# One attention-and-FFN decode step: 64 rows of w_down in one load of eight partitions

## The chip, the cores and the metric

The kernel runs on one core of a Trainium2 chip. The metric is the device time of one execution in microseconds (us), as the median of several runs; lower is better. Times inside an execution come from one profiled run: they count from the start of its span, which is the time from the first to the last instruction.

A core has five engines that work side by side and wait for each other by semaphores: PE (matmul; its weight loads are listed as PEld), DVE (vector), ACT (scalar), POOL (GpSimd) and SP (Sync). All large loads of this kernel are issued by SP and carried by the core's 16 DMA engines, which take them in the order in which SP issued them.

## The reference

One token passes a grouped-query attention over a long cache and then a gated FFN, each with a layer norm in front and a residual behind.

```python
def _A_ref(x, k_cache, v_cache, wq, wo):       # 32 query heads, 4 KV heads, 65536 cached keys, head size 128
    q = (x @ wq) ...                           # D = 1024
    scores = jnp.einsum("bhqd,bhkd->bhqk", q, k) * (Dh ** -0.5)
    p = _softmax(scores, axis=-1)
    o = jnp.einsum("bhqk,bhkd->bhqd", p, v)
    return o... @ wo
def _B_ref(x, w_gate, w_up, w_down):           # F = 3584
    return (_gelu(x @ w_gate) * (x @ w_up)) @ w_down
h  = x + _A_ref(_layernorm(x), k_cache, v_cache, wq, wo)
h2 = h + _B_ref(_layernorm(h), w_gate, w_up, w_down)
```

All tensors are bf16. The caches are 64 MB each, and the five weight matrices 8, 8, 7, 7 and 7 MB.

## The kernel before

**The loads.** Everything that is streamed goes through one SBUF tile, `ring`, of three slots with 32768 bf16 elements on each partition. `load` (line 172) takes the next slot, or a place behind the last load in the same slot when it is given an offset, and issues one DMA on SP (line 179). In order there are `wq`, sixteen loads of the caches, `wo`, `w_gate`, `w_up`, and then `w_down` in five pieces that share one slot. By the count of slots, `wo` and `w_down` use the same slot, and `w_gate` the one after it. A load may not start before the matmuls that read the old contents of its place are done; so the pieces of `w_down` wait for the matmuls of `wo`.

**The layout of w_down.** `w_down` has 3584 rows of 1024 elements. The view `wd_v` puts 28 consecutive rows (FC = 28) on each of 128 partitions. A piece is a range of these 28 places: 16 of them, then 8, then 3; the last place is loaded as two halves of 512 columns, a DMA each, 128 KB over 128 partitions, so 1 KB on each.

**The FFN's activation.** `act_bf` (line 544) holds the 3584 hidden values, 28 on each partition. `padded` (line 235) copies them into `actz`, a tile of [128, 28, 32] that POOL has set to zero, at column 0 of each group of 32, so that a stationary operand is 128 rows by 32 columns with one column that is not zero.

**The first 16 places.** `row_mm` (line 468) multiplies one place with a row of 1024 columns of `w_down`: two matmuls of 512 columns, at one of four column groups of the array (place modulo 4). They add to `at_ps`, the two PSUM banks in which the attention's output and the residual are already summed. Matmuls on four column groups run side by side.

**The end.** `rows_out("sum_r")` copies the two banks to SBUF, DVE one and ACT the other. Eight matmuls with `ones_f` then add the four column groups and lay the result out as eight pieces of 128 columns, in `f_ps` and `fb_ps` (`half_mm`, line 566). The 8 places, the 3 places and the last place are multiplied by `down_rows` (line 570) and added in the same two tiles, in matmuls of 128 columns. After the first half of the last place DVE copies `f_ps` out, after the second ACT copies `fb_ps`, and SP writes the result.

**Fillers.** `keep_busy(n, src)` (line 557) issues n matmuls of 128x128 by 512 columns into `w_ps`, which nobody reads. There are 4 before the first piece of `w_down`, 3 after its 16 places, 4 after the eight matmuls with `ones_f`, and 3 after the 8 places.

**Order.** The framework orders each engine's instructions by a simulation when the kernel is built. `mm` (line 153) passes each matmul through `keep` (line 135), which ties it behind the last one, so PE runs its matmuls in written order. The DMAs of `load`, the POOL instructions and those DVE and ACT instructions that are not wrapped in `dv` or `ac` have no such tie. `seen_by_sync` makes SP wait for the listed loads before the output is written.

```python
for c in range(c0):                                               # c0 = 16
    row_mm(at_ps, actz[:, c, :], wv[:, c, :], c, False, c + 4 >= c0)
keep_busy(3, wv[:, 0, 0:512])
sum_r = rows_out("sum_r")
...
for sz, nb in ((8, 3), (3, 0)):
    wv = load(wd_v[:, c0:c0 + sz, :], c0 * D)
    down_rows(wv, c0, sz, [0, 1])
...
```

Of the kernel before, what the change touches and what calls it, by code (L numbers as in the profile page):

```python
# [9 lines left out]
ALU = mybir.AluOpType  # L10
AX = mybir.AxisListType
BF16 = mybir.dt.bfloat16
F32 = mybir.dt.float32
PSUM = bass.MemoryType.PSUM
# [3 lines left out]
def kernel(  # L18
# [13 lines left out]
    nc = tc.nc  # L32
    P = 128
    D = A_x.shape[-1]
# [4 lines left out]
    F = B_w_gate.shape[1]  # L39
    DC = D // P  # L40
    FC = F // P
# [5 lines left out]
    CW = 16384  # L47
    NSLOT = 3
# [25 lines left out]
    sel = lead.tile([P, 32], F32, name="sel")  # L74
# [12 lines left out]
    ring = chpool.tile([P, NSLOT * 2 * CW], BF16, name="ring")  # L87
    top = ctx.enter_context(tc.tile_pool(name="top", bufs=1))
# [3 lines left out]
    def pt_tile(i, shape, dtype, name):  # L92
        return (lead if i == 0 else top).tile(shape, dtype, name=name, tag=f"pT{i}")
# [50 lines left out]
    def pe(op):  # L144
        return keep(op, "pe")
# [7 lines left out]
    def mm(out, lhsT, rhs, start, stop, loaded=False, tile_position=None, skip_group_check=False):  # L153
        t = nc.tensor
        if not loaded:
            return pe(t.matmul(out, lhsT=lhsT, rhs=rhs, start=start, stop=stop, tile_position=tile_position,  # L156
                               skip_group_check=skip_group_check))
        op = t.add_instruction(mybir.InstMatmult(  # L158
            name=nc.get_next_instruction_name(), engine=t.engine, start_tensor_calc=start, stop_tensor_calc=stop,
            tile_size=(lhsT.shape[0], lhsT.shape[1]), tile_position=tile_position or (0, 0), ldweights=False,  # L160
            bass_skip_group_check=skip_group_check,
            ins=[t.lower_ap(rhs), t.lower_ap(lhsT, for_matmul_weights=True)], outs=[t.lower_ap(out, opt=True)]))
        reuses.add(op.ins.name)
        return pe(op)
# [4 lines left out]
    slot = [NSLOT - 1]  # L169
    loads, pools, last = [], [], {}  # L170

    def load(src, off=0):
        n, w = src.shape[1], src.shape[2]
        if off == 0:
            slot[0] = (slot[0] + 1) % NSLOT
        assert off + n * w <= 2 * CW
        o = slot[0] * 2 * CW + off
        tv = ring[:, o:o + n * w].rearrange("p (n w) -> p n w", w=w)
        loads.append(nc.sync.dma_start(out=tv, in_=src).ins)
        return tv  # L180
# [20 lines left out]
    for bp in range(4):  # L201
        s0 = 64 * (bp // 2) + bp % 2
        nc.vector.tensor_copy(out=esel[:, bp, :, :],
                              in_=ident_bf[:, s0:s0 + 63:2].unsqueeze(1).to_broadcast([P, 4, 32]))

    one = ctx.enter_context(tc.tile_pool(name="one", bufs=1))
# [28 lines left out]
    def padded(i, vec, ncols, name):  # L235
        t = pt_tile(i, [P, ncols, 32], BF16, name)
        pools.append(nc.gpsimd.memset(t[:], 0.0))
        nc.vector.tensor_copy(out=t[:, :, 0], in_=vec)
        return t
# [7 lines left out]
    def evac(dst, src, k):  # L247
        return nc.vector.tensor_copy(out=dst, in_=src) if k % 2 == 0 else nc.scalar.copy(out=dst, in_=src)
# [161 lines left out]
    for n, u in enumerate(units):  # L410
# [24 lines left out]
        if g == 0 and li == NL - 1:  # L435
            softmax_turn(0)
            softmax_bias(0)
            for i, m in zip((NL - 1, 0, 1, 2), (2, 3, 4, 4)):
# [11 lines left out]
                            pattern=[[-1, OQ], [1, P]], channel_multiplier=-OQ)  # L450
# [8 lines left out]
    actx.close()  # L459
    ps_a = ctx.enter_context(tc.tile_pool(name="ps_a", bufs=2, space=PSUM))  # L460
    ps_w = ctx.enter_context(tc.tile_pool(name="ps_w", bufs=2, space=PSUM))
    ps_f = ctx.enter_context(tc.tile_pool(name="ps_f", bufs=1, space=PSUM))
    DS = D // 512

    def row_bank(name):
        return ps_w.tile([P, 512], F32, name=name, tag="w")

    def row_mm(banks, stat, w2, c, first, last):
        g = c % 4
        for s in range(DS):  # L470
            mm(banks[s][32 * g:32 * g + 32, :], stat, w2[:, s * 512:(s + 1) * 512], first, last,
               loaded=(s > 0), tile_position=(0, 32 * g), skip_group_check=True)
# [4 lines left out]
    at_ps = [ps_a.tile([P, 512], F32, name="at_ps", tag="a") for _ in range(DS)]  # L477
    wv = load(wo_v[:])
# [7 lines left out]
    def rows_out(name):  # L486
        t = low.tile([P, DS, 512], F32, name=name, tag="sc0")
        for s in range(DS):
            last["act"] = evac(t[:, s, :], at_ps[s][:], s)
        return t  # L490
# [18 lines left out]
    def turned(banks, name, tag):  # L509
# [2 lines left out]
            nc.vector.transpose(out=t[:, k, :], in_=banks[k][:, 0:HF * 32])  # L512
        return t[:].rearrange("p k (j i) -> p (k j) i", i=32)[:, :, 0]

    g_banks = [row_bank("wg_ps") for _ in range(2)]
    gv = B_w_gate.rearrange("(p c) n -> p c n", c=DC)
    uv = B_w_up.rearrange("(p c) n -> p c n", c=DC)
# [25 lines left out]
    act_bf = top.tile([P, FC], BF16, name="act_bf")  # L543
    nc.vector.tensor_tensor(out=act_bf[:], in0=turned(u_banks, "wu_t", "sc2"), in1=gl[:], op=ALU.mult)

    wd_v = B_w_down.rearrange("(p c) n -> p c n", p=P)
    actz = padded(3, act_bf[:], FC, "actz")
    w_ps = row_bank("w_ps")

    def seen_by_sync(ins):  # L550
        seen = nc.sync.nop()
        for i in ins:
            tc.add_manual_dep(seen.ins, i.name,
                              mybir.DependencyInfo(mybir.DependencyClass.Sync, mybir.DependencyReason.DATA),
                              reason="seen")

    def keep_busy(n, src):
        for i in range(n):
            mm(w_ps[:], ident_bf[:], src, True, True, loaded=(i > 0))

    HW = D // 2
# [8 lines left out]
    def down_rows(wv, c0, n, bs):  # L570
        for cc in range(n):
            c = c0 + cc
            for g in range(4):
                for b in bs:
                    o = (b if len(bs) > 1 else 0) * HW + g * QW
                    half_mm(b, g, actz[:, c, :], wv[:, cc, o:o + QW], False, c + 1 == FC, loaded=(b > bs[0]))

    keep_busy(4, wu[:, 0, 0:512])
    c0 = 16
    wv = load(wd_v[:, 0:c0, :])  # L580
    for c in range(c0):
        row_mm(at_ps, actz[:, c, :], wv[:, c, :], c, False, c + 4 >= c0)
    keep_busy(3, wv[:, 0, 0:512])
    sum_r = rows_out("sum_r")
    for g in range(4):
        for b in range(2):
# [2 lines left out]
    for sz, nb in ((8, 3), (3, 0)):  # L589
        wv = load(wd_v[:, c0:c0 + sz, :], c0 * D)  # L590
# [3 lines left out]
    assert c0 == FC - 1  # L594
    o_b = o_fin[:].rearrange("p (b j) -> p b j", b=2)
    for b, put in ((0, nc.vector.tensor_copy), (1, nc.scalar.copy)):
        wv = load(wd_v[:, c0:FC, b * HW:(b + 1) * HW], c0 * D + b * HW)
        down_rows(wv, c0, 1, [b])
        if b == 1:
            seen_by_sync(loads[-8:] + [last["act"].ins] + [x.ins for x in pools])  # L600
        put(out=o_b[0:97, b, :], in_=halves[b][0:97, :])
    nc.sync.dma_start(out=out[0, 0].rearrange("(b g n) -> g b n", b=2, g=4),
                      in_=o_b[0:97:32, :, :])
# [30 lines left out]
```

## Time and profile before

| | |
|---|---|
| median of three runs | 407.71 us (407.51 to 408.35) |
| the profiled execution | 407.8 us, of which the span is 406.0 us |
| mean granted PE clock | 0.891 of full speed |
| busy: PE, DVE, ACT, POOL | 295.5, 203.8, 40.0, 7.5 us |
| read from HBM | 173.02 MB, 426 GB/s over the span |
| loads of `w_down`: issued | 355.95 us and the 3.6 us after it, five DMAs |
| issue to landing: 16, 8 and 3 places, each half | 39.6, 43.6, 45.0 and 44.8 us |

The time outside the span, 1.8 us, lies before the first and after the last instruction. A matmul's row gives its start and a modelled end; matmuls overlap, so the distance between starts says more than the duration. The granted clock tells how fast PE was allowed to run in a stretch: 1.00 is full speed and 0.50 half.

### The profile page before, as it was taken

How to read it: one execution, taken by the hardware profiler on the slowest of the kernel's cores; microseconds unless marked ns; L12 is line 12 of the kernel's file. 1: busy time of each engine (PE TensorE's matmuls, PEld its weight loads, DVE VectorE, ACT ScalarE, POOL GpSimd, SP SyncE). 2: the span in 40 equal slices, each digit the busy share in tenths (PEclk: the TensorE clock that was granted, in tenths of full speed). 3: DMA queues.
4: the chain of work that ended last, by engine and by line, in shares of the span. 5: the costliest groups of instructions: out<-in, count | busy, mean ns of one | idle time of the engine just before them, and what ended most of it. 6: DMA issues, size and time to landing. Idle time of an engine off the chain costs nothing.

```text
span 406.0 us, 2610 instructions
## 1 busy us (share of the span) xinstructions
PE 295.5 (73%) x1519; PEld 59.4 (15%) x681; DVE 203.8 (50%) x186; ACT 40.0 (10%) x62; POOL 7.5 (2%) x17
## 2 busy tenths in 40 slices
PE   0160777758899695979969957997696999646196
PEld 0110111111111110221111113111110211211012
DVE  0210989999839744971595387609943000220210
ACT  1000000023000031100000302000021100100000
POOL 2000000000000000000000000000010000000000
PEclk9995689987899999769999967899999699886689
DMA  9999999999999999999999999999999999999995
GB/s 413 413 413 471 458 413 415 413 466 452 413 421 420 471 439 413 428 420 471 433 420 428 420 465 433 420 435 420 458 433 420 441 420 458 399 442 447 400 423 225
DMA packets 3631, 173.18 MB, mean 427 GB/s; under 512 B 416, under 2 KB 676, under 8 KB 804
## 3 DMA queue, kind: packets, MB, share of 16 engines
q1 hardware_dynamic: 3612, 173.02, 98.7%
q8 instruction: 8, 0.13, 0.1%
q14 instruction: 3, 0.02, 0.0%
q10 hardware_dynamic: 8, 0.00, 0.0%
HBM read 173.02 MB, written 0.00 MB: 426 GB/s over the span
## 4 chain that ended last, share of the span: by engine, by line
DMA 41%; PE 35%; DVE 21%; ACT 2%; issue 1%; ACTq 0%; DVEq 0%
DMA ring<-in_A_k_cache_dram 30%; DVE ring L288 16%; PE acc_ps L158 16%; DMA ring<-in_B_w_down_dram 11%; PE qk_ps L156 6%; PE qk_ps L158 5%; PE acc_ps L156 5%; DVE mx L313 2%; ACT sc L309 2%; DVE pT L346 1%; PE o_ps L156 1%; PE at_ps L156 1%; DVE acc_sb L369 1%; PE at_ps L158 1%; PE nb_ps L156 0%
## 5 line engine op out<-in xcount | busy, mean ns | idle before, releaser
L288 DVE STREAM_TRANSPOSE ring<-ring 128x2048 uint32<-128x2048 uint32 x64 | 142.6, 2279 | 36.9 <-DMA ring<-in_A_k_cache_dram 36.9
L156 PE MATMUL qk_ps<-ring,wsel 128*128 128x512 bf16 x256 | 107.4, 420 | 50.2 <-DVE ring L288 31.2
L158 PE MATMUL qk_ps<-ring,wsel 128*128 128x512 bf16 x256 | 106.6, 416 | 0.0
L158 PE MATMUL acc_ps<-ring,pT 128*128 128x512 bf16 x384 | 105.1, 383 | 0.0
L156 PEld LDWEIGHTS <-wsel 128*128 128x128 bf16 x256 | 27.1, 106 | 157.3 <-issue 140.4
L156 PE MATMUL acc_ps<-ring,pT 128*128 128x512 bf16 x128 | 49.1, 384 | 0.0
L313 DVE TENSOR_REDUCE mx<-qk_ps 128x1 f32<-128x1024 f32 x16 | 19.5, 1220 | 24.7 <-ACT sc L309 18.7
L346 DVE STREAM_TRANSPOSE pT<-pT 128x1024 bf16<-128x1024 bf16 x16 | 19.3, 1228 | 23.8 <-ACT pT L340 23.8
L309 ACT COPY sc<-qk_ps 128x1024 f32<-128x1024 f32 x12 | 12.1, 1012 | 149.5 <-PE qk_ps L158 149.5
L156 PEld LDWEIGHTS <-pT 128*128 128x128 bf16 x128 | 12.8, 100 | 90.7 <-issue 90.6
L369 DVE COPY acc_sb<-acc_ps 32x512 f32<-32x512 f32 x8 | 5.3, 667 | 29.4 <-PE acc_ps L158 29.3
L340 ACT ACTIVATE pT<-sc,nbias 128x1024 bf16<-128x1024 f32 x12 | 13.7, 1141 | 44.9 <-DVE nbias L332 41.9
L156 PE MATMUL wu_ps<-ring,hnz 128*32 128x448 bf16 x32 | 5.9, 729 | 9.0 <-DMA ring<-in_B_w_up_dram 9.0
L156 PE MATMUL ln_tot<-ln_s,ones_f 128*128 128x1 f32 x8 | 1.9, 312 | 13.5 <-DVE ln_s L210 11.7
L156 PE MATMUL q_ps<-ring,xnz 128*32 128x512 bf16 x32 | 5.0, 598 | 8.9 <-DMA ring<-in_A_wq_dram 8.9
L156 PE MATMUL wg_ps<-ring,hnz 128*32 128x448 bf16 x32 | 5.9, 718 | 7.2 <-DMA ring<-in_B_w_gate_dram 7.2
L156 PE MATMUL o_ps<-sel,acc_sb 128*128 128x8 f32 x32 | 6.6, 335 | 5.8 <-DVE rl L383 5.4
L371 ACT COPY acc_sb<-acc_ps 32x512 f32<-32x512 f32 x8 | 4.6, 578 | 58.6 <-DVE acc_sb L369 58.5
L512 DVE STREAM_TRANSPOSE wu_t<-wu_ps 128x448 f32<-128x448 f32 x2 | 1.2, 630 | 14.2 <-PE wu_ps L156 14.2
L261 DVE STREAM_TRANSPOSE q_t<-q_ps 128x512 f32<-128x512 f32 x2 | 1.3, 694 | 13.8 <-PE q_ps L158 13.8
L512 DVE STREAM_TRANSPOSE wg_t<-wg_ps 128x448 f32<-128x448 f32 x2 | 1.2, 628 | 13.4 <-PE wg_ps L156 13.4
L340 ACT ACTIVATE pT<-qk_ps,nbias 128x1024 bf16<-128x1024 f32 x4 | 4.5, 1114 | 29.8 <-PE acc_ps L158 16.8
(108 smaller groups left out, 94.2 us busy)
## 6 DMA issues: line engine op xcount, KB each, us to landing
ring<-in_B_w_gate_dram SPq DMA_DIRECT2D x1, 7168.0 KB, 35.5
ring<-in_B_w_up_dram SPq DMA_DIRECT2D x1, 7168.0 KB, 38.6
ring<-in_B_w_down_dram SPq DMA_DIRECT2D x1, 4096.0 KB, 39.6
ring<-in_B_w_down_dram SPq DMA_DIRECT2D x1, 2048.0 KB, 43.6
ring<-in_B_w_down_dram SPq DMA_DIRECT2D x1, 768.0 KB, 45.0
ring<-in_B_w_down_dram SPq DMA_DIRECT2D x2, 128.0 KB, 44.8
ring<-in_A_k_cache_dram SPq DMA_DIRECT2D x8, 38.6
ring<-in_A_v_cache_dram SPq DMA_DIRECT2D x8, 34.4
```

The costliest lines, as they stand in the source:

```text
L156: return pe(t.matmul(out, lhsT=lhsT, rhs=rhs, start=start, stop=stop, tile_position=tile_position, skip_group_check=skip_group_check))
L158: op = t.add_instruction(mybir.InstMatmult(name=nc.get_next_instruction_name(), engine=t.engine, start_tensor_calc=start, stop_tensor_calc ...
L261: nc.vector.transpose(out=q_t[:, k, :], in_=q_banks[k])
L288: dv(nc.vector.transpose(out=kt[:, c * w:(c + 1) * w], in_=kt[:, c * w:(c + 1) * w]))
L309: ac(nc.scalar.copy(out=sc[:], in_=flat))
L313: dv(nc.vector.tensor_reduce(out=state[("mx", g)][:, li:li + 1], in_=flat, axis=AX.X, op=ALU.max))
L340: ac(nc.scalar.activation(out=flat, in_=state.pop(("sc", g, li)), func=ACT.Exp, bias=st["nbias"][:, 0:1], scale=scale, accum_out=st["lpart ...
L346: dv(nc.vector.transpose(out=flat, in_=flat))
L369: dv(nc.vector.tensor_copy(out=acc_sb[sl, :], in_=acc[sl, c, :]))
L371: ac(nc.scalar.copy(out=acc_sb[sl, :], in_=acc[sl, c, :]))
L512: nc.vector.transpose(out=t[:, k, :], in_=banks[k][:, 0:HF * 32])
```

## The change

The last place of each partition, 128 rows of `w_down`, is split. The rows of the 64 even partitions stay in the two half-row loads, which now write every second partition (`wv[0:P:2]`). The rows of the 64 odd partitions come in one new DMA: they go to eight partitions (0, 8, ... 56), eight rows of 2 KB on each, 128 KB in all, into the first 8192 elements of the slot after that of `w_down`, which is the slot of `w_gate`. In the program text this DMA stands after the 16 places and before the load of the 8.

The hidden values of the odd partitions must follow their rows. Two small masks are made of `sel`: `part` (which of eight rows a partition's value belongs to) and `even`. `spread`, a 128x128 matrix of ones and zeros, is made on POOL; a matmul of it with `act_q` (the mask times the last hidden value) puts the 64 values onto the eight partitions, in `act_ps`, in a new PSUM pool. `few` is the padded copy of it, and eight `row_mm` multiply it with the eight rows of `lv`, adding to `at_ps` before `sum_r`. In `actz`, the last place is multiplied with `even`.

```diff
+    ps_s = ctx.enter_context(tc.tile_pool(name="ps_s", bufs=1, space=PSUM))
...
+    low_rows = B_w_down.rearrange("(q r c) n -> q r c n", q=KQ, c=2 * FC)[:, :, 2 * FC - 1, :]
...
+    nc.vector.tensor_reduce(out=part[:], in_=sel[:].rearrange("p (x r t) -> p t r x", r=KR, t=2)[:, 1], axis=AX.X, op=ALU.add)
+    nc.vector.tensor_reduce(out=even[:], in_=sel[:, 0::2], axis=AX.X, op=ALU.add)
+    nc.gpsimd.memset(spread[:], 0.0)
+    ones_at = spread[:, 0:8 * KQ:8]
+    nc.gpsimd.memset(ones_at, 1.0)
+    nc.gpsimd.affine_select(out=ones_at, ...)
+    nc.gpsimd.affine_select(out=ones_at, ...)
...
-    actz = padded(3, act_bf[:], FC, "actz")
+    actz = pt_tile(3, [P, FC, 32], BF16, "actz")
+    pools.append(nc.gpsimd.memset(actz[:], 0.0))
+    nc.vector.tensor_copy(out=actz[:, 0:FL, 0], in_=act_bf[:, 0:FL])
+    act_q = one.tile([P, KR], BF16, name="act_q", tag="ln_xc")
+    nc.vector.tensor_tensor(out=act_q[:], in0=part[:], in1=act_bf[:, FL:FC].to_broadcast([P, KR]), op=ALU.mult)
+    nc.vector.tensor_tensor(out=actz[:, FL, 0:1], in0=even[:], in1=act_bf[:, FL:FC], op=ALU.mult)
...
     for c in range(c0):
-        row_mm(at_ps, actz[:, c, :], wv[:, c, :], c, False, c + 4 >= c0)
+        row_mm(at_ps, actz[:, c, :], wv[:, c, :], c, False, False)
+    act_ps = ps_s.tile([P, KR], F32, name="act_ps")
+    mm(act_ps[:], spread[:], act_q[:], True, True)
+    few = padded(1, act_ps[:], KR, "few")
+    at = (slot[0] + 1) % NSLOT * 2 * CW
+    lv = ring[:, at:at + KR * D].rearrange("p (r n) -> p r n", n=D)
+    loads.append(nc.sync.dma_start(out=lv[0:8 * KQ:8], in_=low_rows).ins)
     keep_busy(3, wv[:, 0, 0:512])
+    for r in range(KR):
+        row_mm(at_ps, few[:, r, :], lv[:, r, :], r, False, r + 4 >= KR)
     sum_r = rows_out("sum_r")
...
-        wv = load(wd_v[:, c0:FC, b * HW:(b + 1) * HW], c0 * D + b * HW)
+        o = slot[0] * 2 * CW + c0 * D + b * HW
+        wv = ring[:, o:o + HW].rearrange("p (c n) -> p c n", c=1)
+        loads.append(nc.sync.dma_start(out=wv[0:P:2], in_=wd_v[0:P:2, c0:FC, b * HW:(b + 1) * HW]).ins)
...
-            seen_by_sync(loads[-8:] + [last["act"].ins] + [x.ins for x in pools])
+            seen_by_sync(loads[-9:] + [last["act"].ins] + [x.ins for x in pools])
```

KQ and KR are 8, FL is 27. The bytes read from HBM are the same as before.

More of the change, by code (lines that the diff above doesn't have):

```diff
@@ L513, in turned @@
         return t[:].rearrange("p k (j i) -> p (k j) i", i=32)[:, :, 0]
+    KQ = 8
+    KR = P // 2 // KQ
+    KW = P // KQ
+    assert KQ * KR * 2 == P and 2 * KR == KW and KR * D <= DC * F
+    low_rows = B_w_down.rearrange("(q r c) n -> q r c n", q=KQ, c=2 * FC)[:, :, 2 * FC - 1, :]
+    part = one.tile([P, KR], F32, name="part", tag="gmb")
+    even = top.tile([P, 1], F32, name="even")
+    spread = top.tile([P, P], BF16, name="spread", tag="wo")
+    nc.vector.tensor_reduce(out=part[:], in_=sel[:].rearrange("p (x r t) -> p t r x", r=KR, t=2)[:, 1], axis=AX.X, op=ALU.add)
[3 more added lines that the diff above has]
+    nc.gpsimd.memset(ones_at, 1.0)
+    nc.gpsimd.affine_select(out=ones_at, in_=ones_at, compare_op=ALU.is_ge, fill=0.0, base=0,
+                            pattern=[[-KW, KQ]], channel_multiplier=1)
+    nc.gpsimd.affine_select(out=ones_at, in_=ones_at, compare_op=ALU.is_ge, fill=0.0, base=KW - 1,
+                            pattern=[[KW, KQ]], channel_multiplier=-1)
     g_banks = [row_bank("wg_ps") for _ in range(2)]
@@ L546 @@
     wd_v = B_w_down.rearrange("(p c) n -> p c n", p=P)
-    actz = padded(3, act_bf[:], FC, "actz")
+    FL = FC - 1
+    actz = pt_tile(3, [P, FC, 32], BF16, "actz")
[4 more added lines that the diff above has]
+    nc.vector.tensor_tensor(out=actz[:, FL, 0:1], in0=even[:], in1=act_bf[:, FL:FC], op=ALU.mult)
     w_ps = row_bank("w_ps")
```

## The prediction

> **What bounds the kernel now.** I read the page, then the chain of work that ended last, the timeline of the last 11 us, the waits, the timelines of POOL and SP, and the windows. The DMA engines are busy nearly all the span; the chain's last link is a load of w_down (start, duration):
>
> ```profile
> DMA  9999999999999999999999999999999999999995
> ...
> 358.13 44.71 DMA ring<-in_B_w_down_dram
> ```
>
> It landed at 402.84. The timeline of PE (start, us, operation) shows what was done meanwhile:
>
> ```profile
> 395.56 0.41 PE L156 MATMUL at_ps<-ring,actz 128*32 128x512 bf16 x4 [0.26 <-DMA ring<-in_B_w_down_dram]
> ...
> 397.07 0.41 PE L158 MATMUL at_ps<-ring,actz 128*32 128x512 bf16 x4
> 397.41 0.39 PE L156 MATMUL w_ps<-ring,ident_bf 128*128 128x512 bf16 x1
> ...
> 398.27 0.45 PE L156 MATMUL f_ps<-sum_r,ones_f 128*32 128x128 f32 x8
> ...
> 398.87 0.39 PE L156 MATMUL w_ps<-ring,ident_bf 128*128 128x512 bf16 x1
> ...
> 400.41 0.24 PE L156 MATMUL f_ps<-ring,actz 128*32 128x128 bf16 x4 [0.51 <-DMA ring<-in_B_w_down_dram]
> ...
> 401.43 0.39 PE L156 MATMUL w_ps<-ring,ident_bf 128*128 128x512 bf16 x1
> ...
> 402.23 0.24 PE L156 MATMUL f_ps<-ring,actz 128*32 128x128 bf16 x4
> ...
> 402.88 0.24 PE L156 MATMUL fb_ps<-ring,actz 128*32 128x128 bf16 x4
> ```
>
> PE begins each piece 0.04 us after it landed (395.52, 400.37, 402.19, 402.84 by the trace's semaphore records) and fills the time between with fillers. Its spare time is small: the fillers from 398.87 would let the 8 places start at about 399.89 instead of 400.41 (0.52 us spare), those from 401.43 end as the 3 places land (none), and before the last half some 0.25 us are spare. After 402.88 the copy, the output and the end of the span take 3.1 us, in any version.
>
> The second reading is how instruction streams are ordered. Two answers, POOL and SP:
>
> ```profile
> 340.39 0.31 POOL L237 MEMSET hnz<- 128x256 bf16 x1 [5.95 <-PE acc_ps L158]
> 347.30 0.84 POOL L237 MEMSET actz<- 128x896 bf16 x1 [6.59 <-PE acc_ps L158]
> 362.13 0.56 POOL L226 TENSOR_TENSOR ln_rstd<-ln_ve,neg_half 128x1 f32<-128x1 f32 x1 [13.98 <-DVE ln_ve L224]
> ...
> 355.95 3.58 SPq L179 DMA_DIRECT2D ring<-in_B_w_down_dram x5
> ```
>
> The second layer norm's power (called at line 503) is written before the memsets of `hnz` (504) and `actz` (547), yet both run earlier, at 340 and 347, each when its buffer came free. So an engine's stream is in order of readiness, not of the text, where nothing ties it. PE is tied; SP's DMAs are not. All five pieces left together, as the matmuls of wo (352.61 to 357.4) freed their places.
>
> **The change, part by part.** *Masks and `spread`*: two DVE reduces (0.16 to 0.23 us each, by lines 195 and 210), and on POOL two memsets (0.21 and 0.1), two selects (0.30 each, by the identity's) and the memset of `few` (0.31). POOL is idle for 14.0 us before 362.13 and DVE for 13.4 before 376.58. Nothing; without that cover they would delay the layer norm by 1.2 us, still inside PE's 7.2 us wait for w_gate. *Two multiplies on DVE* after `actz` (0.2 each): if the first 16 places waited for them too, PE would start at 395.75, +0.2 at most. One more semaphore in SP's last wait: nothing, its load is used 5 us earlier.
>
> *PE's new work*: after 397.07 come a 128x8 matmul, the old three fillers beside the copy to `few` (DVE, 0.25 by the copies at 351.63 and 352.26, from 0.26 after the matmul), and 16 matmuls of 512 columns, four groups of 0.215 us. `sum_r` waits for the last.
>
> *The two halves*: 64 packets of 1 KB each instead of 128. The old halves landed 0.34 us apart, so each takes 0.17 less; 0.34 in sum.
>
> *The new load* decides. Its place is the slot of w_gate: its first 8192 elements were read by w_gate's first three chunks, about 369.0 to 371.9. The 8 places, the 3 places and the halves, written after it, are ready at about 357, when the matmuls of wo are done. By the POOL rows, SP's stream gets them first: 16, 8, 3, half, half, and the new load last, issued after 371.9 but behind all of w_down in the DMA engines. PE, tied to the text, reaches the new rows at about 398.3 and stands there, with the 8, the 3 and the halves unread behind it.
>
> When does it land? A DMA engine carries 16 KB of it if eight engines share it: a 16 KB packet took 0.61 us in the trace's packet records, two old halves 0.68; I take 0.65. With the 0.34 saved that is 0.31 after the old last half on the same engine. That half's sixteen increments came in two groups, seven at 400.71 to 401.39 and nine at 402.30 to 402.84. So it lands at 401.7 if its engines are all early ones, 403.15 if the latest is among them; I take 403.0, since nine of sixteen are late. Before, the load of x_row into four partitions left eight packets (four of data, four increments), so I take it that eight partitions mean eight engines. A rule of the Trainium skill speaks against this load: "SBUF — State Buffer", Door 1, puts partitions 0 and 32, 8 and 40 and so on onto shared ports, so that eight partitions reach four. No row here shows that; by it the load would take twice as long and land at 403.7.
>
> From there PE is alone on the path. First new matmul 403.04; to the start of the last group 0.65; to the matmuls with ones 1.20 (397.07 to 398.27); those 0.60; four fillers 1.02 (398.87 to 399.89); the 8 places 1.02 (400.41 to 401.43); three fillers 0.80; the 3 places 0.34 and one half 0.06. Sum 5.69: the last half starts at 408.73 instead of 402.88, +5.85 us.
>
> *The clock*: PE then idles from 398.2 to 403.0. The windows (us; PE, PEld, DVE, ACT, POOL busy; granted clock; DMA share; GB/s):
>
> ```profile
> 375.90:379.31 3.41, 1.01 (x12) 0.00 (x0) 2.26 (x8) 0.23 (x1) 0.00 (x0) 1.00 1.09 471
> 386.14:389.55 3.41, 3.41 (x24) 0.51 (x12) 0.00 (x0) 0.00 (x0) 0.00 (x0) 0.50 1.00 432
> ```
>
> Clock steps lie on a grid of 3.41 us: after a window with 1.01 us of PE the clock halved at 379.31, and the full window to 389.55 brought it back. The window 399.8 to 403.2 would be almost empty, so the new matmuls run at half speed. If that lasts to 406.6, the rows, the copy's start and the ones cost about 1.3 us more; if to 410.0 (the window to 406.6 would hold some 2.5 us of PE; one with 2.95 raised the clock, and none here between 1.8 and 2.9 settles it), about 2.9 with fillers and 8 places. If the grid falls otherwise, 0. I take 1.5. In sum +7.35.
>
> The profiled run took 407.8 (span 406.0), 0.1 above the median of 407.71: 407.71 + 7.35 = 415.1. With the load at 401.7 and no clock loss it is +4.55, 412.3. With 403.15 and the long loss it is +8.9, 416.6. The three runs lay from 0.2 below to 0.64 above their median, so the range is 412.1 to 417.2.
>
> **Rivals.** *(1) The load leaves in written order*, between the 16 and the 8. For it: the text, and that nothing in the loads before was ever overtaken (each waits for its slot in turn, so they could not). Against: the POOL rows. It would be issued about 372, long before the engines run dry at 395, and land by 396.2. PE: matmul for `few` 397.41, fillers to 398.3, new rows 398.34 with the last group at 398.98, `sum_r` to 400.18, ones to 400.78, fillers to 401.80, 8 places to 402.82, fillers to 403.62, 3 places and a half to 404.02: +1.14, since 1.9 us of new work meets 0.75 of spare time. 408.85.
>
> *(2) Not slower.* The load goes in written order to the eight engines that run 1.3 to 2 us ahead; the late ones lose 8 KB, 0.34 us, and the last half lands at 402.5: 407.4. For it: the DMA engines' uneven end (seven and nine above). It decides only if PE is at the halves by 402.5; by (1) it comes at 404.0, so the new matmuls would have to fit into the fillers' time, against the tie of line 135.
>
> *(3) The load is spread over sixteen engines*, not the eight that it says: 0.33 less, 414.8, inside the forecast's range.
>
> **How the numbers follow.** Load last: 0.83, with (3) in it; its range 412.1 to 417.2 holds it 24 in 25. Written order: 0.13, two thirds of it above 408.5. Not slower: 0.04, a quarter of it beyond the bound. The measurement can tell about 0.2%, 0.8 us, from no change. Slower 0.92, same 0.07, faster 0.01. The range 412.1 to 417.2 holds 0.8; the rest is mostly (1).
>
> **What would show it.** Right: SP's timeline with the new issue alone near 372, after five others; PE waiting 4 to 5 us for a load of w_down before a `few` matmul at 401.7 to 403.2; a half clock after it; 5.7 us or more from there to the last half. Wrong: a `few` matmul at 398.3 with no DMA wait means (1); if the last matmul then still starts by 402.9, PE's spare time was larger than I read.

## The result, and the profile after

The changed kernel took 410.98 us (410.33 to 411.21, four runs) beside 408.03 (407.51 to 408.37, four runs) of the kernel before: a ratio of 1.0071, 95% interval 1.0053 to 1.0089. It is 2.95 us slower, where 7.35 was forecast. Its profiled execution took 411.17 us, with a span of 408.4.

The page's row of busy DMA engines, and four links of the chain that ended last:

```profile
DMA  9999999999999999999999999999999999999984
...
393.09 0.40 PE wu_ps L158 x4
393.50 0.76 SPq L613
394.32 8.63 DMA ring<-in_B_w_down_dram
402.99 0.24 PE f_ps L156 x4
```

Before, the chain's last transfer was issued at 358.13. Now the chain runs over the last matmul of w_up and the issue of the new load (line 613) to the load of the 8 places, which left SP only at 394.32. SP's own timeline (start, us; several issues together are one row) and SP's longest wait (us in total, times, longest):

```profile
355.82 0.33 SPq L179 DMA_DIRECT2D ring<-in_B_w_down_dram  x1
393.50 0.76 SPq L613 DMA_DIRECT2D ring<-in_B_w_down_dram  x1
394.32 0.87 SPq L179 DMA_DIRECT2D ring<-in_B_w_down_dram  x2
395.24 1.15 SPq L632 DMA_DIRECT2D ring<-in_B_w_down_dram  x2
```

```profile
SPq L613 <- PE wu_ps L158: 24.5, 1, 24.5
```

SP kept the written order: 16 places, new load, 8, 3, halves. The new load waited 24.5 us for the last matmul of w_up, and the 8 and 3 places, free to go at 357, stood behind it. The windows (columns as in the prediction; the last two are DMA share and GB/s, and count each packet in the window in which it starts) show what that did. First before, then after:

```profile
393.00:394.00 1.00, 0.89 (x12) 0.10 (x1) 0.43 (x1) 0.00 (x0) 0.00 (x0) 1.00 1.07 459
394.00:395.00 1.00, 0.73 (x4) 0.00 (x0) 0.95 (x3) 0.00 (x0) 0.00 (x0) 1.00 0.77 328
395.00:396.00 1.00, 0.74 (x11) 0.32 (x8) 0.23 (x1) 0.00 (x0) 0.00 (x0) 1.00 1.03 442
```

```profile
393.00:394.00 1.00, 0.61 (x9) 0.10 (x1) 0.85 (x2) 0.00 (x0) 0.00 (x0) 1.00 0.61 262
394.00:395.00 1.00, 0.88 (x4) 0.06 (x1) 0.85 (x5) 0.00 (x0) 0.00 (x0) 1.00 0.00 0
395.00:396.00 1.00, 0.50 (x12) 0.26 (x8) 0.00 (x0) 0.00 (x0) 0.00 (x0) 1.00 1.05 264
```

From 394 to 395 no packet started; some of the expectations below call this the empty second, and here it is called the gap. It was not empty: by the packet records eight engines finished their part of the 16 places from 393.50 to 393.85, and the other eight carried packets begun by 393.84 until 394.56 to 395.06. The new load, issued at 393.50, moved its first packet at 395.00, 1.5 us later. Counted over the packets' own times, the sixteen engines were busy for 0.69, 0.37 and 0.62 of the three windows, so each stood idle for 1.3 us on average. PE's timeline:

```profile
395.50 0.41 PE L156 MATMUL at_ps<-ring,actz 128*32 128x512 bf16 x4 [0.63 <-DMA ring<-in_B_w_down_dram]
...
397.35 0.18 PE L156 MATMUL act_ps<-act_q,spread 128*128 128x8 bf16 x1
...
398.13 0.41 PE L156 MATMUL at_ps<-ring,few 128*32 128x512 bf16 x4
...
399.98 0.45 PE L156 MATMUL f_ps<-sum_r,ones_f 128*32 128x128 f32 x8 [0.80 <-DVE sum_r L248]
...
402.99 0.24 PE L156 MATMUL f_ps<-ring,actz 128*32 128x128 bf16 x4 [1.37 <-DMA ring<-in_B_w_down_dram]
...
404.82 0.24 PE L156 MATMUL f_ps<-ring,actz 128*32 128x128 bf16 x4
...
405.20 0.25 PE L156 MATMUL fb_ps<-ring,actz 128*32 128x128 bf16 x4
```

The `few` matmuls start at 398.13 with no DMA wait: the new load had landed at 397.08 (its last semaphore record). The wait is at the 8 places, 1.37 us, which start 2.58 later than before (400.41); the last half starts 2.32 later (402.88).

The sixteen increments of the 8 places' semaphore, one from each DMA engine, say more: fifteen came from 401.34 to 401.80 and one at 402.95. The packet records show a 16 KB packet of another queue, "instruction", at 399.24 for 1.01 us: an instruction fetch, taken here to be PE's. The records name no engine; that it sat on the late one follows from the packets' succession: one that starts as the fetch ends, at 400.24, took 1.08 us instead of 0.61, and the chain behind it, packet after packet, ends last. Before, the same fetch came at 398.73 and, by the increments, met an engine that ran ahead: eight of sixteen were early for the 8 places, seven for the 3 places. It held nobody up, because the engines that ran behind set the end. In the changed kernel no engine runs ahead any more: fifteen increments lie within 0.46 us.

So there were three suspects: the order on SP with the gap, the fetch, and PE's new work, which the wait may hide.

### The profile page after: what moved, and what is told of

Its sections match the earlier page's. It is cut to its first block, busy times and chain, and to the rows that moved or that the text cites. A ratio compares the mean times of both kernels' runs of the same rounds, so it can differ in the third digit from the quotient of the medians.

```text
span 408.4 us, 2652 instructions
## 1 busy us (share of the span) xinstructions
PE 294.7 (72%) x1536; PEld 58.7 (14%) x690; DVE 204.3 (50%) x191; ACT 40.0 (10%) x62; POOL 8.6 (2%) x22
## 4 chain that ended last, share of the span: by engine, by line
DMA 41%; PE 37%; DVE 18%; ACT 2%; issue 1%; SPq 0%; ACTq 0%
DMA ring<-in_A_k_cache_dram 30%; PE acc_ps L158 15%; DVE ring L288 14%; DMA ring<-in_B_w_up_dram 10%; PE qk_ps L156 6%; PE qk_ps L158 6%; PE acc_ps L156 5%; DVE mx L313 2%; DMA ring<-in_B_w_down_dram 2%; ACT sc L309 1%; DVE pT L346 1%; PE wu_ps L156 1%; PE wu_ps L158 1%; PE o_ps L156 0%; PE nb_ps L156 0%
```

## The experiments

Eleven kernels ran. Each edit is against the changed kernel unless said; every ratio is to the kernel before on the same chip.

### The load where its partitions are contiguous

```diff
-    ones_at = spread[:, 0:8 * KQ:8]
+    ones_at = spread[:, 0:KQ]
-    loads.append(nc.sync.dma_start(out=lv[0:8 * KQ:8], in_=low_rows).ins)
+    loads.append(nc.sync.dma_start(out=lv[0:KQ], in_=low_rows).ins)
```

> The changed kernel, with the new load on partitions 0 to 7 instead of 0, 8, ... 56 (and the matrix spread made to match). Theory A (the new load waits for the last matmul of w_up because of its stepped partitions, and the 8, the 3 and the halves stand behind it in SP's stream until the DMA engines have run dry): the new load is issued at about 372 instead of 393.5, no dry second at 394, the 8 places land near 400.9; PE's own new work is then the bound, the 8 places start near 401.7 and the last half near 404.0; about +1.15 us on the kernel before, a ratio of 1.0028. Rival B (PE's new work alone makes the whole loss): nothing changes against the changed kernel, ratio 1.007.

409.88 us, ratio 1.0046 (1.0033 to 1.0058). SP's timeline, then three windows:

```profile
373.28 0.85 SPq L613 DMA_DIRECT2D ring<-in_B_w_down_dram  x1
374.19 0.87 SPq L179 DMA_DIRECT2D ring<-in_B_w_down_dram  x2
```

```profile
393.00:394.00 1.00, 0.99 (x12) 0.08 (x1) 0.32 (x1) 0.00 (x0) 0.00 (x0) 1.00 0.96 295
394.00:395.00 1.00, 0.57 (x2) 0.02 (x1) 0.97 (x3) 0.00 (x0) 0.00 (x0) 1.00 0.82 205
395.00:396.00 1.00, 0.40 (x2) 0.09 (x1) 0.41 (x4) 0.00 (x0) 0.00 (x0) 1.00 0.82 252
```

On partitions 0 to 7 the load leaves 20 us earlier, just after w_gate's first chunks are read. It is still issued ahead of the 8 and 3 places, so the written order holds here too. The same place in the ring, addressed with a step of eight partitions, had waited for the last matmul of w_up, which reads another slot: that wait comes from the stepped address, not from the data. The gap is gone, but a new loss replaced it: the three windows have 205 to 295 GB/s, 251 on average, where before they had 410. The 32 KB packets of the 16 places beside the 2 KB packets of the new load took 1778 to 1868 ns instead of 1213. PE:

```profile
396.80 0.41 PE L156 MATMUL at_ps<-ring,actz 128*32 128x512 bf16 x4 [1.40 <-DMA ring<-in_B_w_down_dram]
```

The 16 places start 1.24 later than before. From there no DMA wait follows, and the last half starts at 405.01, 8.21 after them, where before it was 7.32: the other +0.9 is PE's new work.

### The load without PE's use of it

```diff
-    act_ps = ps_s.tile([P, KR], F32, name="act_ps")
-    mm(act_ps[:], spread[:], act_q[:], True, True)
-    few = padded(1, act_ps[:], KR, "few")
...
-    for r in range(KR):
-        row_mm(at_ps, few[:, r, :], lv[:, r, :], r, False, r + 4 >= KR)
```

> The changed kernel without PE's new work: the matmul of spread, the copy to few and the sixteen matmuls with the new rows are left out, so the rows of the odd partitions are loaded and not used. Theory A: the late issue stays, so the 8 places land at 401.8, or near 403 if the code fetch of PE falls into that stretch again; the last half starts between 404.1 and 405.2; ratio 1.003 to 1.0065. Rival B: PE is as before, ratio 1.000.

411.78 us, ratio 1.0101 (1.0085 to 1.0116), above Theory A: with less work it is 0.8 us slower than the whole change (the two intervals just touch). PE's row at the 8 places, and the window after it:

```profile
402.79 0.30 PE L156 MATMUL f_ps<-ring,actz 128*32 128x128 bf16 x4 [3.03 <-DMA ring<-in_B_w_down_dram]
```

```profile
402.60:406.00 3.40, 2.88 (x66) 1.45 (x32) 0.00 (x0) 0.00 (x0) 0.00 (x0) 0.50 0.20 75
```

The 8 places land as late as in the changed kernel (fifteen by 401.68, one at 402.75), so the load and its place on SP make the wait without PE's new work. The late engine again follows a fetch (398.98, 1.03 us). PE stood still for 3.03 us and was then granted half its clock to 406.0; the last half starts at 406.41. In the changed kernel PE's new work shortens that wait to 1.37.

### The load without PE's use of it, PE kept busy

The kernel above with `keep_busy(16, ...)` instead of `keep_busy(4, ...)` ahead of the 8 places.

> The new load without PE's use of it (the odd rows of the last place left out, as in the run of the load alone), but with 16 instead of 4 unused 128x512 matmuls ahead of the 8 places, some 2.6 us more of work in a wait of 3.03 us. Theory (the load alone was 0.8 us slower than the whole change because PE stood idle and its clock fell to 0.50 at 402.6): the granted clock stays 1.00 to the end, the 8 places still start near 402.8 with the DMA, and the last half comes at 405.0 to 405.2 instead of 406.41, so the median falls by about 1.2 us from 411.8 to 410.6, ratio near 1.007. Rival (the clock is not the cause): 411.8 again, ratio 1.010.

410.44 us, ratio 1.0071 (1.0059 to 1.0082). The window and PE's row:

```profile
402.60:406.00 3.40, 1.96 (x69) 1.03 (x33) 0.00 (x0) 0.00 (x0) 0.00 (x0) 1.00 0.58 230
```

```profile
404.44 0.24 PE L156 MATMUL f_ps<-ring,actz 128*32 128x128 bf16 x4 [1.28 <-DMA ring<-in_B_w_down_dram]
```

The clock stays full and the median falls by 1.34. The landmarks of this execution do not match the expected 402.8 and 405.1: its new load left 1.2 us later than in the kernel above, at 394.75, and everything after it shifted too. It waits for w_up's last matmul, and PE was slower there: from 389 to 391 its granted clock was 0.50, in the kernel above 1.00. The page "TensorE: Matmul & The Clock Gate" of the Trainium skill, section "Part 1", says that the gate falls to half after an idle window of some 3.4 us and returns after some 3.4 us of work. In the kernel above the half clock from 402.60 to 406.00 fits the second length; the idle stretch before it, 3.03 us, was shorter than the first.

So the load and the order cost about 2.7 us by themselves, the fetch's delay included (one increment came at 404.40, fifteen by 402.83). That is nearly all that the change costs.

### PE's new work without the load

```diff
-    loads.append(nc.sync.dma_start(out=lv[0:8 * KQ:8], in_=low_rows).ins)
```

The `few` matmuls read what w_gate left in the slot; the 64 odd rows are left out.

> The changed kernel without the new load: few is multiplied with what w_gate left in that place, so the contribution of the odd partitions is not the reference's. Theory A: SP's stream is free, the 8 and the 3 places are issued near 357 as before, and only PE's new work is left: the 8 places start near 401.6 and the last half near 404.0, +1.15 us, ratio 1.0028. Rival B: the whole loss is here, ratio 1.007.

409.45 us (408.61 to 409.92), ratio 1.0038 (1.0025 to 1.005). In the profiled execution, the fastest of the five, the 8 places start without a DMA wait:

```profile
401.29 0.24 PE L156 MATMUL f_ps<-ring,actz 128*32 128x128 bf16 x4
```

They had landed at 400.30. The last half starts at 403.46, 8.22 after the first of the 16 places, where before it was 7.32: +0.9. The median is 1.7 above before; what the slower executions add was not seen in a trace. So PE's new work costs 0.9 to 1.7 us by itself.

### The halves without their odd partitions

The kernel before, with only the even partitions of the last place loaded (`wv[0:P:2]`) and the odd ones left out: the change's one saving by itself.

> The kernel before with one part of the change: the two halves load only the even partitions, and the odd partitions' last rows are left out. Their stepped partitions should make them wait for the last matmul of w_up too, but behind nothing that is missing: issued at 393.5 to 395 while the 8 and the 3 places still run. The last half lands up to 0.34 us earlier: 0.0 to -0.3 us, ratio 0.9993 to 1.000 by both theories. If the late issue of the halves itself costs time, over 1.001.

407.66 us (eleven runs), ratio 0.9996 (0.9988 to 1.0005): nothing. The last half starts at 402.81 instead of 402.88. The halves' stepped address made them wait on SP until 394.23 here too, without harm, since nothing was queued behind them.

### The order on SP alone

The kernel above, with the two half loads written ahead of the 8 and the 3 places, and `keep_busy(12, ...)` ahead of the 8 places. No new load, no `few`.

> No new load and no new matmuls: the kernel before with only the halves' even partitions (the odd rows of the last place are left out), and these two half loads written ahead of the 8 and 3 places, so that on SP the 8 and 3 places stand behind a load that waits for the last matmul of w_up; 12 unused matmuls instead of 4 keep PE at work meanwhile. Theory (the standing behind is by itself most of the changed kernel's price): the DMA engines have nothing to move in 394 to 395, the 8 places start 1.0 to 2.3 later than the 400.53 of the kernel with the halves alone, and the last half with them: 408.7 to 410.0, ratio 1.0025 to 1.006; at the upper end if the instruction packet near 399 meets one of the engines that carry the 8 places. Rival (PE's new work or the new load's packets make the price, the order alone is worth nothing): 407.7, ratio 1.000.

412.96 us (410.44 to 413.72), ratio 1.0109 (1.0088 to 1.013). SP, three windows, PE, and a later window:

```profile
394.95 1.17 SPq L599 DMA_DIRECT2D ring<-in_B_w_down_dram  x2
396.17 1.06 SPq L179 DMA_DIRECT2D ring<-in_B_w_down_dram  x2
```

```profile
394.00:395.00 1.00, 0.92 (x12) 0.10 (x1) 0.40 (x1) 0.00 (x0) 0.00 (x0) 1.00 0.00 0
395.00:396.00 1.00, 0.65 (x3) 0.00 (x0) 0.96 (x3) 0.00 (x0) 0.00 (x0) 1.00 0.00 0
396.00:397.00 1.00, 0.90 (x14) 0.26 (x8) 0.26 (x3) 0.00 (x0) 0.00 (x0) 1.00 0.24 76
```

```profile
405.05 0.25 PE L156 MATMUL f_ps<-ring,actz 128*32 128x128 bf16 x4 [2.56 <-DMA ring<-in_B_w_down_dram]
```

```profile
406.00:407.00 1.00, 0.71 (x28) 0.43 (x9) 0.00 (x0) 0.00 (x0) 0.00 (x0) 0.50 0.03 12
```

Both theories said less. Two issues stand ahead of the 8 places instead of one. By the packet records no load moves from 395.12 to 396.28, then only the halves' 1 KB packets do, and the first packet of the 8 places moves at 397.41. The first 16 KB packets after this took 1.0 to 1.6 us instead of 0.61, with no other load beside them; why is open. Fifteen increments came by 403.62, the sixteenth at 405.01: again one engine is late after an instruction fetch (398.30, 0.93 us). PE, idle for 2.56 us, lost half its clock. The last half starts at 408.76, 5.95 later than in the kernel above: the 8 places start 4.52 later, and 1.43 comes after them, at half clock. This is the slowest of the six executions; the fastest, 410.44, is still 2.8 above that kernel. So the stall by order, with neither the new rows nor their matmuls, costs about as much as the whole change even there, and more at the median. That its size depends on how long the issues ahead take is likely, but not shown apart from the late end of w_up (halves issued at 394.95; the clock was 0.50 from 389 to 391 here too).

### The instruction fetch moved

```diff
+    early_ps = ps_m.tile([P, 8], F32, name="early_ps", tag="misc")
+    for i in range(110):
+        mm(early_ps[:], ident_bf[:], hnz[:, 0, 0:8], True, True, loaded=(i > 0))
     g_banks = [row_bank("wg_ps") for _ in range(2)]
```

> 110 tiny matmuls (128x8, result unused) go onto PE ahead of w_gate's matmuls, where PE waits for data; nothing else differs from the changed kernel. The packet of 16 KB that PE's queue of instructions fetched at 399.24 in the changed kernel, near PE's 2056th instruction, should then come some 110 instructions earlier, near 394. Theory (that packet, 1.0 us on one of sixteen engines, held the sixteenth landing of the 8 places at 402.95 while fifteen were there by 401.80): all sixteen land by 401.9, the 8 places start near 401.9 instead of 402.99, the last half near 404.1, the median some 1.1 us under the changed kernel's: ratio to before near 1.0045. Rival (the late landing comes from the empty second and not from the fetch): the 8 places start at 402.9 as before, ratio 1.007.

409.74 us (409.04 to 409.97), ratio 1.0048 (1.0034 to 1.0061). A window and PE:

```profile
394.00:395.00 1.00, 0.89 (x3) 0.00 (x0) 0.93 (x6) 0.00 (x0) 0.00 (x0) 1.00 0.01 0
```

```profile
401.93 0.24 PE L156 MATMUL f_ps<-ring,actz 128*32 128x128 bf16 x4 [0.48 <-DMA ring<-in_B_w_down_dram]
```

The fetches came at 377.25 and 403.26, not near 394: how many instructions lie between two was misjudged. But none fell among the 8 places' packets, and the gap stayed. All sixteen increments came by 401.9, the 8 places started at 401.93, and the last half at 404.17, 1.03 earlier than in the changed kernel. That confirms the fetch as about 1.1 us of the price in the profiled execution, and, since added PE instructions moved it, as PE's. The median is 1.2 lower, with intervals that overlap a little. What is left, 2.05 at the median, is little more than PE's new work costs without the load (1.7).

### The load last, as the forecast had it

SP's order written out as 16, 8, 3, both halves, new load; PE's order unchanged.

> The order that the forecast assumed, written out: SP issues the pieces of 16, 8 and 3 places, both halves, and then the new load; PE's order is the changed kernel's. By the forecast's sum the matmuls of `few` wait 4 to 5 us for the new load, until about 403.0, and the last half's matmul comes at 408.7 with TensorE's clock full (5.85 later than before) or 410.2 at half clock (7.35 later): 413.6 to 415.1 us, ratio 1.014 to 1.018. Theory from the runs so far (one reason for the changed kernel's price is the 8 and 3 places standing behind the new load): DMA has no empty second at 394, the 8 and 3 places land as early as before, and the whole price is PE's wait. Rival: the order on SP is worth nothing, and the time is the changed kernel's, 1.007.

417.40 us (416.61 to 417.92), ratio 1.0233 (1.0219 to 1.0246). SP's timeline, PE's row and two windows:

```profile
356.68 1.67 SPq L179 DMA_DIRECT2D ring<-in_B_w_down_dram  x3
394.39 1.19 SPq L620 DMA_DIRECT2D ring<-in_B_w_down_dram  x2
395.63 0.73 SPq L622 DMA_DIRECT2D ring<-in_B_w_down_dram  x1
```

```profile
403.55 0.62 PE L156 MATMUL at_ps<-ring,few 128*32 128x512 bf16 x4 [5.00 <-DMA ring<-in_B_w_down_dram]
```

```profile
403.20:406.60 3.40, 2.25 (x24) 0.64 (x19) 0.69 (x1) 0.59 (x1) 0.00 (x0) 0.50 0.00 0
406.60:410.00 3.40, 3.07 (x55) 1.15 (x29) 0.00 (x0) 0.00 (x0) 0.00 (x0) 0.50 0.00 0
```

This is the forecast's mechanism: a wait of 5.00 us at the first `few` matmul (4 to 5 forecast), to 403.55 (403.04 forecast), then PE alone. The last half starts at 412.10, 8.55 after the first `few` matmul. The forecast's sum of 5.69 at full clock and 2.9 for the longer half clock is 8.59. It had taken 1.5 instead of 2.9, so even in its own case it was too low: 415.1 against 417.40, just above its range.

### Other shapes of the same load

The contiguous version with `KQ = 32` (two rows each on partitions 0 to 31) and `KQ = 16`, and one with a row each on partitions 0 to 31 and 64 to 95, in two loads.

> The same 64 rows on 32 partitions side by side with two rows each, instead of eight with eight; PE runs 4 matmuls of 32x512 on them instead of 16. Theory (the eight packed partitions slowed all transfers from 393 to 397 because they are two of SBUF's ports): 32 partitions side by side are eight ports, SP issues the load near 373 as it did there, the rate in 393 to 397 is that of before (over 400 GB/s but for one second), the new load's packets take under 100 ns, the 16 places start near 395.4 instead of 396.8, the 8 places are bound by PE near 400.9, and the last half comes near 403.0: 408.0 to 409.0 us, ratio 1.000 to 1.003. Rival (rows scattered over other partitions' packets disturb by themselves, or the order on SP decides): the rates of the packed run, ratio 1.0045 or more.

> The same 64 rows of w_down on sixteen partitions side by side (0 to 15) with four rows each; sixteen DMA engines take part, as they did with 32 partitions, and SP issues the load at about 371 to 373. Between eight partitions (32 KB packets of the 16 places beside it 1778 to 1868 ns, undisturbed 1213; 16 places start 396.80; ratio 1.0046) and 32 partitions (1440 to 1599 ns; 396.37; ratio 1.0028). Theory (what counts is how many of SBUF's ports the load reaches: two with 8 partitions, eight with 32, four here): 32 KB packets of 1550 to 1750 ns, the 16 places start near 396.6, ratio 1.003 to 1.0045. Rival (what counts is that small packets run beside the large ones, or that eight engines carry them instead of sixteen): packets as with 32 partitions, 1440 to 1600 ns, ratio 1.0028.

> The same 64 rows one to a partition, in two loads of 32 partitions (0 to 31 and 64 to 95); PE runs 2 matmuls of 32x512 on them instead of 16. Theory (ports): these partitions reach all sixteen ports, as the 128-partition loads do, so the 32 KB packets of the 16 places stay at 1213 ns, the 16 places start near 395.4, the 8 places are bound by PE at about 400.9 and the last half comes near 403.1: about 408.0, ratio 1.000 to 1.002. Rival (the small packets themselves): 32 KB packets of 1440 ns and more again, the 16 places start near 396.4, ratio 1.0025 or more, and a second load on SP adds to it.

| partitions | `few` matmuls | 32 KB packets beside the small ones, ns | 16 places start | ratio (interval) |
|---|---|---|---|---|
| 8 | 16 | 1778 to 1868 | 396.80 | 1.0046 (1.0033 to 1.0058) |
| 16 | 8 | 1432 to 1527, one 2005 | 396.84 | 1.0049 (1.0037 to 1.0061) |
| 32 | 4 | 1440 to 1599 | 396.37 | 1.0028 (1.0017 to 1.0039) |
| 64, in two loads | 2 | 1322 to 1472 | 395.90 | 1.0023 (1.0015 to 1.0032) |

The 64-row load slows the transfers beside it in each shape, most with eight partitions and least with 64; 16 and 32 hardly differ in their packets. The Trainium skill's page "SBUF — State Buffer", section "Door 1", puts these partitions on two, four, eight and all sixteen of SBUF's ports. If ports alone decided, the last row would show 1213 ns, and the second would lie clearly above the third; by the packets neither holds. Small packets beside large ones cost something even on all ports. In the eight-partition version eight engines carry the load, in the others sixteen, so its larger delay has two possible causes. From 16 partitions on the ratios fall with the `few` matmuls too and do not separate the transfers from PE's work. The traces do: from the first of the 16 places to the last half it takes 8.21, 7.78, 7.75 and 7.69 us (before: 7.32), so PE's new work is 0.89, 0.46, 0.43 and 0.37, and the 16 places start 1.24, 1.28, 0.81 and 0.34 late. In the last version, with no gap and two `few` matmuls, PE sets the end: its 16 places start without a DMA wait (they had landed at 395.82, 0.30 later than before), and so do its 8 places, at 401.42. None beats the kernel before.

## Why the prediction was wrong

**The direction and the bound.** Slower by over 0.2% had 0.92, and it was slower; that PE would wait for a load of w_down was right too. But the wait was for the 8 places and not for the new rows, so the hit on the direction is in good part luck. The time, 410.98, lies below the range (412.1 to 417.2) and above rival (1) (408.85).

**The failed step: the order on SP.** The forecast had the 8 places, the 3 places and the halves leave ahead of the new load: "By the POOL rows, SP's stream gets them first". It did not: the new load left in written place, at 393.50, and they left behind it, from 394.32. So the wait of 4 to 5 us for the new load never came; with the order written out as forecast, it did (5.00). The readings of POOL said nothing on SP here; POOL's `few` memset (358.76) still overtook the layer norm's power (363.18) in the changed kernel. Rival (1) had the argument, that no load had ever been overtaken on SP, and was given 0.13. Why the framework reorders POOL and kept SP in order, no run here shows.

**The second failed step, in rival (1) too: "issued about 372".** The data allowed that, as the contiguous versions show (370.5 to 373.3). The stepped address waited for w_up's last matmul, 393.50. Rival (1) had the load leave long before the engines run dry at 395, and land by 396.2. It left at 393.50 and moved its first packet at 395.00, when eight engines had been done since 393.85 at the latest; it landed at 397.08. With PE walking as rival (1) said (`few` at 398.13, 398.34 told), the path moved to the 8 places, which no forecast had late.

**PE's new work.** Rival (1)'s +1.14 was +0.9 measured without the load. In the changed kernel PE stood ready for the 8 places at 401.62 (402.99 less the wait of 1.37), 1.21 after their start before. Their fifteen punctual increments came by 401.80, so beside PE's new work the gap adds only some 0.2, and the fetch the other 1.15. The prices overlap and do not add: 1.7 for PE's work alone, 2.7 for the load with PE kept busy, 2.95 for both.

**The clock.** No half clock came; the wait was 1.37 us and not 5. Where PE did wait 2.56 to 5.00 us, it came, and with the load last its term, 1.5 us, was mis-sized: 2.9 measured (8.55 less the 5.69 of the other terms).

**The rule on ports.** By the Trainium skill's page "SBUF — State Buffer", section "Door 1", the prediction said, the load would take twice as long, by its estimate. In the changed kernel its 2 KB packets took 84 ns at the median (the slowest 571), beside 76 for each 2 KB of an undisturbed 32 KB packet (1213 / 16): no doubling shows. Nothing on PE waited for them.

**The halves.** A saving of 0.34 was priced; by itself it gave nothing measurable.

The sum for the changed kernel's profiled execution: the 8 places land 2.58 later; 1.15 of it is the one engine behind the fetch, 1.43 the late issue, with the new load's own packets and the long first packets after the gap. After them 0.26 is won back, since the last pieces have landed by the time PE reaches them. That leaves +2.32 at the last half. This execution also spent 1.0 us more outside its span than before (2.77 against 1.8), which the other three (1.7 to 1.9) did not; their spans were longer instead (408.6 to 409.5).

## What to carry to other kernels

Before moving a small load ahead in a queue, ask when its own wait ends and what stands behind it: a transfer that may start late must be issued late, and one issue that waits can leave the DMA engines idle, here for 1.3 us on average. Two causes of delay that meet at one wait overlap: removing one uncovers the other. Look at how the destination is addressed: a stepped range of partitions made a DMA wait for matmuls that read other places of the tile, and a contiguous range did not. And a piece of work off the path can be what keeps PE's clock up, so removing it may cost time.

## What the runs showed of the hardware

- An instruction fetch of PE is a 16 KB packet of about 0.9 to 1.1 us on one of the sixteen DMA engines. A load lands with its slowest engine, so a fetch at the wrong moment delayed the 8 places by 1.15 us; moved away, it cost nothing.
- A load's first packet moved 1.2 to 1.5 us after its issue began (393.50 to 395.00 in the changed kernel, 396.17 to 397.41 with the order alone). An issue that waits until the engines run out therefore leaves them idle.
- 2 KB packets running beside 32 KB packets lengthened the latter from 1213 to between 1322 and 1868 ns (one: 2005). Why is open; the number of ports does not explain it alone.
- Waits of PE of 2.56, 3.03 and 5.00 us each led to half the clock; waits of 1.28, 1.37 and 1.40 us did not.
